# Strassen's algorithm for the states' first product, these tokens moved to the end, sums of w_in during batch 7

## Chip, cores, metric

The kernel runs on one core of one Trainium2 chip. The metric is the time on the device in microseconds. Most statements below need a second figure, the span that the profile gives from the core's first to last instruction; it lies 1.7 to 2.8 us under the time. All arithmetic here is float32 on TensorE.

## The reference

```python
# x: (8, 8, 512, 64), state: (8, 8, 32, 64), w_in: (512, 2048), w_out: (2048, 512)
a      = softmax(scale * x @ state.T)        # 512 tokens of a batch look at 32 states
xread  = a @ state
a2     = softmax(scale * state @ x.T)        # 32 states look at 512 tokens
sread  = a2 @ x
t      = concatenate([xread, sread])         # (8 batches * (512 + 32) tokens, 512)
h      = t @ w_in                            # the first product
out    = (h * sigmoid(1.702 * h)) @ w_out    # the second product
```

There are 8 x 512 "x tokens" and 8 x 32 = 256 "states' tokens". All 256 of these go through the two products together.

## The kernel before

The x tokens of batches 2 to 7 already use Strassen's algorithm (Winograd's form, 7 products and 15 sums) in both products; the states' tokens use it in the second product alone. Their first product is plain: 16 blocks of the hidden dimension, for each 4 matmul instructions over the 512 inputs, 256 columns wide.

```python
def up(key, f, ntok, lhs, rhs, spare=False):
    hps = ... psH.tile([P, ntok], FP32, tag="h", name=f"h_{key}_{f}")
    for i in range(n):                                   # n = 4 for the states
        nc.tensor.matmul(hps, lhs[i], rhs[i], start=(i == 0), stop=(i == n - 1))
    ...
    nc.scalar.activation(out=G[key, f // 2][:, f % 2, :ntok], in_=hps, func=AF.Gelu_apprx_sigmoid)

def up_s(f):
    up("sr", f, B * Ns, [w_in_of(k, f) for k in range(NPR)],
       [srT[:, k].rearrange("p b n -> p (b n)") for k in range(NPR)])
# ...
srT = konst.tile([P, NPR, B, Ns], FP32, name="srT")      # the states' tokens, batch by batch
# ... the end of the program:
for b in range(1, B):
    ahead = b + 1 < B
    if not ahead:                                        # the states ahead of batch 7
        for f in range(NF):
            up_s(f)
            ...                                          # sums for the second product
        strassen("sr", B * Ns, lambda r, n: out_s[nb * r.start : nb * r.stop, :, n])
    slots = att_slots(b + 1) if ahead else [[]]          # the next batch's attention, in 14 slots
    if b > 1:
        slots[0].insert(0, (up_strassen(b), ()))
    strassen(b, S, lambda r, n: out_x[b, r, :, n].rearrange("r q n -> q r n"), slots)
```

`strassen` is the second product: 7 products named by the PSUM bank in which they lie (x, y, x, y, z, y, z), a slot after every 8 instructions, and the sums of w_out made once. `up_strassen` is the first product of one batch; it leaves its last block of work to be done in slot 0, inside the second product.

Of the kernel before, what the change touches and what calls it, by code (L numbers as in the profile page):

```python
# [10 lines left out]
FP32 = mybir.dt.float32  # L11
# [3 lines left out]
ALU = mybir.AluOpType  # L15
# [5 lines left out]
def kernel(  # L21
# [30 lines left out]
    nc = tc.nc  # L52

    B, H, S, D = x.shape
# [179 lines left out]
        done["credit"] -= n  # L234
        round_to(done["b"] + n)

    def w_in_of(k, f):
        c, o = divmod(P * f, FC)
        return w_in[c][:, k, o : o + P]


    srT = konst.tile([P, NPR, B, Ns], FP32, name="srT")

# [174 lines left out]
    def up(key, f, ntok, lhs, rhs, spare=False):  # L418
        hps = att_ps([P, ntok], f"h_{key}_{f}") if spare else psH.tile([P, ntok], FP32, tag="h", name=f"h_{key}_{f}")
        n = len(lhs)  # L420
        for i in range(n):
            nc.tensor.matmul(hps, lhs[i], rhs[i], start=(i == 0), stop=(i == n - 1))  # L422
        if f % 2 == 0:
            G[key, f // 2] = free.pop(0)
        nc.scalar.activation(out=G[key, f // 2][:, f % 2, :ntok], in_=hps, func=AF.Gelu_apprx_sigmoid)  # L425
# [3 lines left out]
        m = A[b]["M", c]  # L429
        up(b, f, S, [m[:, g, o : o + P] for g in range(NG)], [A[b]["aT"][:, g] for g in range(NG)], spare)  # L430

    def up_s(f):
        up(
            "sr", f, B * Ns,
            [w_in_of(k, f) for k in range(NPR)],
            [srT[:, k].rearrange("p b n -> p (b n)") for k in range(NPR)],
        )

    O = {}

    def down(key, r, fs, dst, last):
# [19 lines left out]
    def quarters(key, u, ntok):  # L461

        g, half = G[key, u], ntok // 2
        return g[:, :, :half], g[:, :, half:ntok]

    def s12(key, u, ntok):

        half = ntok // 2
        (a11, a21), (_, a22) = quarters(key, u, ntok), quarters(key, HF // 2 + u, ntok)
        s1, s2 = S1[:, 2 * u : 2 * u + 2, :half], S2[:, 2 * u : 2 * u + 2, :half]  # L470
        nc.vector.tensor_tensor(out=s1, in0=a21, in1=a22, op=ALU.add)  # L471
        nc.vector.tensor_tensor(out=s2, in0=s1, in1=a11, op=ALU.subtract)

    def s3(key, u, ntok):

        a11, a21 = quarters(key, u, ntok)
        nc.vector.tensor_tensor(out=a21, in0=a11, in1=a21, op=ALU.subtract)

    def strassen(key, ntok, dst, slots=None):
        half = ntok // 2  # L480
        nb = half // P
        B11, B21, B22 = w_out[:, :HF, :HN], w_out[:, HF:, :HN], w_out[:, HF:, HN:]
        T3 = w_out[:, :HF, HN:]
        A = lambda i, k: [quarters(key, (HF * k + f) // 2, ntok)[i][:, f % 2] for f in range(HF)]
        S = lambda t: [t[:, f, :half] for f in range(HF)]
        todo = list(slots or [])

        def bank(name):
            return psO.tile([P, nb, HN], FP32, tag="o", name=f"{name}_{key}")

        def product(ps, lhs, rhs, first):
            for r in range(nb):
                for f in range(HF):
                    nc.tensor.matmul(  # L494
                        ps[:, r], lhs[f][:, P * r : P * (r + 1)], rhs[:, f],
                        start=(first and r == 0 and f == 0), stop=(f == HF - 1), skip_group_check=True,
                    )
                if todo:
                    for fn, args in todo.pop(0):
                        fn(*args)  # L500

        def kept(t):
            return t[:, : nb * HN].rearrange("p (r n) -> p r n", r=nb)

        def store(i, k, ps, with_):

            o = opool.tile([P, nb, HN], FP32, tag="osb", name=f"osb_{key}_{i}{k}")
            if with_ is None:
                nc.scalar.copy(o, ps)
            else:  # L510
                nc.vector.tensor_tensor(out=o, in0=ps, in1=with_, op=ALU.add)  # L511
            nc.sync.dma_start(dst(slice(nb * i, nb * (i + 1)), slice(HN * k, HN * (k + 1))), o)

        k1, k2, k3 = kept(p1), kept(u2), kept(u3)
        X = bank("x")
        product(X, A(0, 0), B11, True)
        nc.scalar.copy(k1, X)
        Y = bank("y")
        product(Y, S(S2), T2, True)
        nc.vector.tensor_tensor(out=k2, in0=Y, in1=k1, op=ALU.add)  # L520
        product(X, A(0, 1), B21, False)
        store(0, 0, X, None)
        for u in range(HF // 2):
            a12 = quarters(key, HF // 2 + u, ntok)[0]
            nc.vector.tensor_tensor(out=a12, in0=a12, in1=S2[:, 2 * u : 2 * u + 2, :half], op=ALU.subtract)
        product(Y, A(1, 0), T3, False)
        nc.vector.tensor_tensor(out=k3, in0=Y, in1=k1, op=ALU.add)
        free.extend(G[key, u] for u in range(HF // 2))
        Z = bank("z")
        product(Z, S(S1), T1, True)  # L530
        store(1, 1, Z, k3)
        product(Y, A(1, 1), T4, False)
        store(1, 0, Y, k1)
        product(Z, A(0, 1), B22, False)
        store(0, 1, Z, k2)
        free.extend(G[key, u] for u in range(HF // 2, HF))
# [23 lines left out]
            for c in range(2):  # L560
                nc.vector.tensor_tensor(out=t[:, c], in0=a["M", c][:, 1], in1=a["S2"][:, c], op=ALU.subtract)

    def up_strassen(b):

        a = A[b]
        b11, b22 = a["aT"][:, 0, :QT], a["aT"][:, 1, QT:]
        b21 = a["aT"][:, 1, :QT]
        t1, t2, t3, t4 = a["T"]
        banks = {}

        def product(u, bank, lhs, rhs, first):
            if first:
                pool, tag = (psH, "h") if bank == "x" else (psO, "o")
                banks[bank, u] = pool.tile([P, 2, QT], FP32, tag=tag, name=f"up{bank}_{b}_{u}")
            ps = banks[bank, u]
            for k in range(2):
                o = 2 * P * (u % 2) + P * k
                nc.tensor.matmul(  # L578
                    ps[:, k], lhs[:, o : o + P], rhs, start=(first and k == 0), stop=True, skip_group_check=True
                )  # L580
            return ps

        def gelu(dst, src):
            nc.scalar.activation(out=dst, in_=src, func=AF.Gelu_apprx_sigmoid)  # L584

        def add(ps, x, dst):
            nc.vector.tensor_tensor(out=dst, in0=ps, in1=x, op=ALU.add)  # L587

        def parts(u):
            c = u // 2  # L590
            return a["M", c], a["M", 2 + c], a["S1"][:, c], a["S2"][:, c], a["S4"][:, c]


        def begin(u):
            lo, hi, m1, m2, m4 = parts(u)
            G[b, u], G[b, NU + u] = free.pop(0), free.pop(0)
            _, c12 = quarters(b, u, S)
            c21, _ = quarters(b, NU + u, S)
            nc.scalar.copy(c21, product(u, "x", lo[:, 0], b11, True))
            add(product(u, "y", m2, t2, True), c21, c12)  # L600

        def middle(u):
            lo, hi, m1, m2, m4 = parts(u)
            c11, c12 = quarters(b, u, S)
            c21, c22 = quarters(b, NU + u, S)
            z = product(u, "z", m1, t1, True)
            gelu(c11, product(u, "x", lo[:, 1], b21, False))
            add(product(u, "y", hi[:, 0], t3, False), c21, c22)
            add(z, c22, c22)
            gelu(c22, c22)  # L610

        def end(u):
            lo, hi, m1, m2, m4 = parts(u)
            c11, c12 = quarters(b, u, S)
            c21, c22 = quarters(b, NU + u, S)
            add(product(u, "y", hi[:, 1], t4, False), c21, c21)
            gelu(c21, c21)
            add(product(u, "z", m4, b22, False), c12, c12)
            gelu(c12, c12)
            if u:  # L620
                s12(b, u - 1, S)

        for u in range(NU):
            begin(u)
            if u:
                end(u - 1)
            middle(u)

        def rest():
            end(NU - 1)  # L630
            s12(b, NU - 1, S)
            for u in range(NU):
                s3(b, u, S)

        return rest

# [112 lines left out]
    T_of(B12, B22, B12)  # L749
    T_of(T4, B21, T2)  # L750

    nb = P // Ns
    for b in range(1, B):
        ahead = b + 1 < B
        if not ahead:
            for f in range(NF):
                up_s(f)
                if f > HF and f % 2:
                    s12("sr", (f - HF) // 2, B * Ns)
                    s3("sr", (f - HF) // 2, B * Ns)  # L760
            strassen("sr", B * Ns, lambda r, n: out_s[nb * r.start : nb * r.stop, :, n])
        slots = att_slots(b + 1) if ahead else [[]]
        if b > 1:
            slots[0].insert(0, (up_strassen(b), ()))
        strassen(b, S, lambda r, n: out_x[b, r, :, n].rearrange("r q n -> q r n"), slots)
        if b + 2 < B:
            load_state(b + 2)
            load_x(b + 2)


# [28 lines left out]
```

## Time and profile before

| | before |
|---|---|
| time, three runs | 755.9, 756.31, 757.17 us |
| span of the profiled run | 755.7 us |
| TensorE / VectorE / ScalarE busy | 98% / 55% / 31% |
| states' first product | 128 records of 256 columns, 27.6 us |
| last store | 256 KB, 2.21 us from issue to last landing |

One thing is to be known about the times first: they are of two kinds. In some executions the trace has a stretch of 3413 ns at half clock some 41 to 43 us after the start, behind a pause of 2.1 us in which TensorE waits for ScalarE. The page of the profiled run before shows it only when asked for short stretches (columns: stretch, its length, busy time of PE, PEld, DVE, ACT and POOL with instructions, granted clock, share of the DMA engines, GB/s):

```profile
38.00:42.00 4.00, 1.98 (x17) 0.31 (x16) 3.93 (x7) 3.69 (x7) 0.00 (x0) 1.00 0.00 0
42.00:46.00 4.00, 3.90 (x6) 1.79 (x7) 3.90 (x9) 1.43 (x4) 0.00 (x0) 0.62 0.01 2
```

Executions with it have a mean clock of 0.996 to 0.998 and take about 1.7 us more; those without have 0.999 or 1.0. Both kinds are counted as fast. So I compare executions of the same kind, and call those without the stretch "clean".

### The profile page before, as it was taken

Reading aid. Unit: us, or ns where it says so; the run is one execution under the profiler, and the core shown is the slowest. Engines: PE = TensorE matmul, PEld = TensorE weight load, DVE = VectorE, ACT = ScalarE, POOL = GpSimd, SP = SyncE. Lnnn points to the kernel's source line nnn. Section 1 sums busy time; section 2 is a strip of 40 time slices with the busy share of each in tenths; the row PEclk is TensorE's granted clock in tenths of the full one; section 3 lists DMA queues with packets and bytes.
Section 4 is the critical chain, followed back from the end, with each engine's and each line's share of the span. In section 5 each row is a group of like instructions: output and inputs, shape, how many; then the busy total and the mean of one; then the engine's idle time right before and its main releaser. Section 6 shows DMA issues by size and latency. Waiting matters only on the chain.

```text
span 755.7 us, 9853 instructions
## 1 busy us (share of the span) xinstructions
PE 743.6 (98%) x4171; PEld 563.8 (75%) x4171; DVE 413.9 (55%) x712; ACT 231.7 (31%) x411; POOL 0.8 (0%) x8
## 2 busy tenths in 40 slices
PE   8989999999999999999999999999999999999997
PEld 3423454467888878887788788887888778888886
DVE  5999699632646373555637264638364550225511
ACT  4667611022324241433134232424142312104200
POOL 0000000000000000000000000000000000000000
PEclk9999999999999999999999999999999999999999
DMA  9811245010030000300030003000130000000001
GB/s 233 330 61 52 84 152 159 0 57 1 28 78 10 1 15 29 74 1 15 29 74 0 1 29 87 3 1 15 38 64 1 15 29 15 0 22 8 0 15 42
DMA packets 48763, 35.22 MB, mean 47 GB/s; under 512 B 36432, under 2 KB 44112, under 8 KB 48720
## 3 DMA queue, kind: packets, MB, share of 16 engines
q1 hardware_dynamic: 48720, 34.61, 15.9%
q8 instruction: 32, 0.52, 0.3%
q14 instruction: 11, 0.09, 0.0%
HBM read 25.69 MB, written 8.91 MB: 46 GB/s over the span
## 4 chain that ended last, share of the span: by engine, by line
PE 96%; SPq 2%; ACT 1%; DMA 1%; issue 0%; DVE 0%; ACTq 0%
PE y L494 19%; PE z L494 13%; PE x L494 13%; PE upy L578 8%; PE h L422 8%; PE o L447 7%; PE upx L578 5%; PE upz L578 5%; PE M L276 4%; PE h_sr L422 4%; PE xT L258 2%; PE y_sr L494 1%; SPq L131 1%; PE sr L371 1%; PE s L276 1%; PE z_sr L494 1%
## 5 line engine op out<-in xcount | busy, mean ns | idle before, releaser
L494 PE MATMUL x<-w_out,g 128*128 128x256 f32 x448 | 100.2, 379 | 0.0
L494 PEld LDWEIGHTS x<-w_out,g 128*128 128x128 f32 x448 | 84.2, 190 | 11.4 <-ACT osb L454 0.2
L587 DVE TENSOR_TENSOR g<-upy,g 128x512 f32<-128x512 f32 x72 | 48.1, 689 | 68.7 <-PE upy L578 68.7
L584 ACT ACTIVATE g<-g 128x512 f32<-128x512 f32 x72 | 44.8, 630 | 84.8 <-DVE g L587 84.8
L422 PE MATMUL h<-aT,M 128*128 128x512 f32 x128 | 59.9, 614 | 4.4 <-ACT M L351 4.4
L351 ACT COPY M<-M 128x512 f32<-128x512 f32 x64 | 33.2, 596 | 95.1 <-PE M L276 95.1
L422 PEld LDWEIGHTS h<-aT,M 128*128 128x128 f32 x128 | 24.2, 194 | 37.9 <-issue 25.5
L494 PE MATMUL z<-sums,later 128*128 128x256 f32 x224 | 51.1, 382 | 0.0
L494 PE MATMUL z<-w_out,g 128*128 128x256 f32 x224 | 50.8, 382 | 0.0
L494 PE MATMUL y<-sums,later 128*128 128x256 f32 x224 | 50.5, 379 | 0.0
L494 PE MATMUL y<-sums,g 128*128 128x256 f32 x224 | 50.5, 379 | 0.0
L494 PE MATMUL y<-w_out,g 128*128 128x256 f32 x224 | 50.1, 382 | 0.0
L494 PEld LDWEIGHTS y<-w_out,g 128*128 128x128 f32 x224 | 42.1, 190 | 10.5 <-issue 5.0
L494 PEld LDWEIGHTS z<-sums,later 128*128 128x128 f32 x224 | 42.1, 190 | 10.5 <-issue 5.0
L578 PE MATMUL upx<-aT,M 128*128 128x256 f32 x192 | 49.3, 379 | 0.0
L578 PE MATMUL upy<-ta,M 128*128 128x256 f32 x192 | 49.3, 379 | 0.0
L494 PEld LDWEIGHTS z<-w_out,g 128*128 128x128 f32 x224 | 41.6, 190 | 6.2
L494 PEld LDWEIGHTS y<-sums,g 128*128 128x128 f32 x224 | 41.6, 190 | 5.2
L494 PEld LDWEIGHTS y<-sums,later 128*128 128x128 f32 x224 | 41.6, 190 | 5.2
L471 DVE TENSOR_TENSOR later<-g,g 128x512 f32<-128x512 f32 (+1 forms) x32 | 20.8, 651 | 40.7 <-ACT g L425 40.7
L511 DVE TENSOR_TENSOR osb<-z,later 128x512 f32<-128x512 f32 x14 | 9.7, 692 | 60.2 <-PE z L494 60.2
L578 PEld LDWEIGHTS upx<-aT,M 128*128 128x128 f32 x192 | 36.5, 190 | 5.0
(130 smaller groups left out, 1023.0 us busy)
## 6 DMA issues: line engine op xcount, KB each, us to landing
later<-in_moe_w_out_dram SPq DMA_DIRECT2D x16, 512.0 KB
out_dram<-osb SPq DMA_DIRECT2D x32, 256.0 KB
xn<-in_x_dram SPq DMA_DIRECT2D x28, 256.0 KB
w_out<-in_moe_w_in_dram SPq DMA_DIRECT2D x12, 512.0 KB
later<-in_moe_w_in_dram SPq DMA_DIRECT2D x4, 512.0 KB
sums<-in_x_dram SPq DMA_DIRECT2D x4, 256.0 KB
stn<-in_state_dram SPq DMA_DIRECT2D x16, 32.0 KB
out_dram<-osb_sr SPq DMA_DIRECT2D x4, 128.0 KB
```

Of the source, the lines that this page charges most:

```text
L131: nc.sync.dma_start(xn[b][:, c], x_v[b, c])
L258: nc.tensor.transpose(ps[:, c], x_heads(b, c, j), ident)
L276: nc.tensor.matmul(ps[g][st], A[b]["stT"][rows, st], rhs(rows, j), start=True, stop=True)
L351: nc.scalar.copy(m[:, g], ps[g])
L422: nc.tensor.matmul(hps, lhs[i], rhs[i], start=(i == 0), stop=(i == n - 1))
L447: nc.tensor.matmul(ops, G[key, f // 2][:, f % 2, P * r : P * (r + 1)], w_out[:, f], start=(f == 0), stop=(f == NF - 1))
L471: nc.vector.tensor_tensor(out=s1, in0=a21, in1=a22, op=ALU.add)
L494: nc.tensor.matmul(ps[:, r], lhs[f][:, P * r : P * (r + 1)], rhs[:, f], start=(first and r == 0 and f == 0), stop=(f == HF - 1), skip_grou ...
L511: nc.vector.tensor_tensor(out=o, in0=ps, in1=with_, op=ALU.add)
L578: nc.tensor.matmul(ps[:, k], lhs[:, o : o + P], rhs, start=(first and k == 0), stop=True, skip_group_check=True)
L584: nc.scalar.activation(out=dst, in_=src, func=AF.Gelu_apprx_sigmoid)
L587: nc.vector.tensor_tensor(out=dst, in0=ps, in1=x, op=ALU.add)
```

## The change

The intent: 7 products in place of 8 for the states' first product as well. They need the four quarters of w_in added and subtracted; VectorE is to do that while TensorE works on batch 7. For this the states' tokens go behind batch 7, and `up_strassen` is made general (a list of pieces of the inner dimension, as the states have two where a batch has one). The diff, cut to its core:

```diff
+    def sr_sums():
+        mm = [mpool.tile([P, NG, FC], FP32, tag="M", name=f"ws_{i}") for i in range(4)]
+        s1, s2 = mm[:2], mm[2:]
+        ...                                             # s4 in xT, t1..t4 in e1, quarters of srT and w_in
+        for c in range(2):
+            steps.append((tt, (s1[c], hi[c][0], hi[c][1], ALU.add)))
+            steps.append((tt, (s2[c], s1[c], lo[c][0])))
+            steps.append((tt, (hi[c][0], lo[c][0], hi[c][0])))
+            steps.append((tt, (s4[c], lo[c][1], s2[c])))
+        steps += [(tt, v) for v in ((t1, r12, r11), (t2, r22, t1), (t3, r22, r12), (t4, r21, t2))]
@@ in product() of up_strassen
+            n = len(lhs)
             for k in range(2):
                 o = 2 * P * (u % 2) + P * k
-                nc.tensor.matmul(
-                    ps[:, k], lhs[:, o : o + P], rhs, start=(first and k == 0), stop=True, skip_group_check=True
-                )
+                for i in range(n):
+                    nc.tensor.matmul(
+                        ps[:, k], lhs[i][:, o : o + P], rhs[i],
+                        start=(first and k == 0 and i == 0), stop=(i == n - 1), skip_group_check=True,
+                    )
@@ the end of the program
         if not ahead:
-            for f in range(NF):
-                up_s(f)
-                ...
-            strassen("sr", B * Ns, lambda r, n: out_s[nb * r.start : nb * r.stop, :, n])
+            steps, left, right = sr_sums()
+            for i, step in enumerate(steps):
+                slots[1 + i].append(step)
         strassen(b, S, lambda r, n: out_x[b, r, :, n].rearrange("r q n -> q r n"), slots)
...
+    strassen(
+        "sr", B * Ns, lambda r, n: out_s[nb * r.start : nb * r.stop, :, n],
+        [[(up_strassen("sr", B * Ns, left, right), ())]],
+    )
```

More of the change, by code (lines that the diff above doesn't have):

```diff
@@ L235, in pace @@
         round_to(done["b"] + n)
-    def w_in_of(k, f):
-        c, o = divmod(P * f, FC)
-        return w_in[c][:, k, o : o + P]
     srT = konst.tile([P, NPR, B, Ns], FP32, name="srT")
@@ L430, in up_x @@
         up(b, f, S, [m[:, g, o : o + P] for g in range(NG)], [A[b]["aT"][:, g] for g in range(NG)], spare)
-    def up_s(f):
-        up(
-            "sr", f, B * Ns,
-            [w_in_of(k, f) for k in range(NPR)],
-            [srT[:, k].rearrange("p b n -> p (b n)") for k in range(NPR)],
-        )
     O = {}
@@ L561, in up_sums, with parts_x, left @@
                 nc.vector.tensor_tensor(out=t[:, c], in0=a["M", c][:, 1], in1=a["S2"][:, c], op=ALU.subtract)
-    def up_strassen(b):
+    def parts_x(b):
         a = A[b]
-        b11, b22 = a["aT"][:, 0, :QT], a["aT"][:, 1, QT:]
-        b21 = a["aT"][:, 1, :QT]
-        t1, t2, t3, t4 = a["T"]
+        t1, t2, t3, t4 = ([t] for t in a["T"])
+        r11, r21, r22 = [a["aT"][:, 0, :QT]], [a["aT"][:, 1, :QT]], [a["aT"][:, 1, QT:]]
+        def left(u):
+            c = u // 2
+            lo, hi = a["M", c], a["M", 2 + c]
+            return [lo[:, 0]], [lo[:, 1]], [hi[:, 0]], [hi[:, 1]], [a["S1"][:, c]], [a["S2"][:, c]], [a["S4"][:, c]]
+        return left, (r11, r21, r22, t1, t2, t3, t4)
@@ new lines, in sr_sums, with tt, each, left @@
+    def sr_sums():
+        HT, HK = B * Ns // 2, NPR // 2
+        mm = [mpool.tile([P, NG, FC], FP32, tag="M", name=f"ws_{i}") for i in range(4)]
+        s1, s2 = mm[:2], mm[2:]
+        t = apool.tile([P, NPR, S], FP32, tag="xT", name="ws4")
+        s4 = [t[:, HK * c : HK * (c + 1)] for c in range(2)]
+        t = apool.tile([P, NG, NB, Ns], FP32, tag="e1", name="ta_sr").rearrange("p g i n -> p (g i n)")
+        t1, t2, t3, t4 = ts = [t[:, HK * HT * i : HK * HT * (i + 1)].rearrange("p (k t) -> p k t", k=HK) for i in range(4)]
+        sT = srT.rearrange("p k b n -> p k (b n)")
+        r11, r12, r21, r22 = (sT[:, HK * i : HK * (i + 1), HT * k : HT * (k + 1)] for i in range(2) for k in range(2))
+        lo = [[w_in[c][:, HK * i : HK * (i + 1)] for i in range(2)] for c in range(2)]
+        hi = [[w_in[2 + c][:, HK * i : HK * (i + 1)] for i in range(2)] for c in range(2)]
+        def tt(out, x0, x1, op=ALU.subtract):
+            nc.vector.tensor_tensor(out=out, in0=x0, in1=x1, op=op)
+        steps = []
+        for c in range(2):
[4 more added lines that the diff above has]
+        steps += [(tt, v) for v in ((t1, r12, r11), (t2, r22, t1), (t3, r22, r12), (t4, r21, t2))]
+        def each(v):
+            return [v[:, k] for k in range(HK)]
+        def left(u):
+            c = u // 2
+            return [each(v) for v in (lo[c][0], lo[c][1], hi[c][0], hi[c][1], s1[c], s2[c], s4[c])]
+        return steps, left, [each(v) for v in (r11, r21, r22, *ts)]
@@ L569, in up_strassen @@
+    def up_strassen(b, ntok, left, right):
+        QT = ntok // 2
+        b11, b21, b22, t1, t2, t3, t4 = right
         banks = {}
@@ L575, in product @@
             ps = banks[bank, u]
+            n = len(lhs)
             for k in range(2):
                 o = 2 * P * (u % 2) + P * k
-                nc.tensor.matmul(
-                    ps[:, k], lhs[:, o : o + P], rhs, start=(first and k == 0), stop=True, skip_group_check=True
-                )
+                for i in range(n):
[3 more added lines that the diff above has]
+                    )
             return ps
@@ L587, in add @@
             nc.vector.tensor_tensor(out=dst, in0=ps, in1=x, op=ALU.add)
-        def parts(u):
-            c = u // 2
-            return a["M", c], a["M", 2 + c], a["S1"][:, c], a["S2"][:, c], a["S4"][:, c]
         def begin(u):
-            lo, hi, m1, m2, m4 = parts(u)
+            l11, l12, l21, l22, m1, m2, m4 = left(u)
             G[b, u], G[b, NU + u] = free.pop(0), free.pop(0)
-            _, c12 = quarters(b, u, S)
-            c21, _ = quarters(b, NU + u, S)
-            nc.scalar.copy(c21, product(u, "x", lo[:, 0], b11, True))
+            _, c12 = quarters(b, u, ntok)
+            c21, _ = quarters(b, NU + u, ntok)
+            nc.scalar.copy(c21, product(u, "x", l11, b11, True))
             add(product(u, "y", m2, t2, True), c21, c12)
         def middle(u):
-            lo, hi, m1, m2, m4 = parts(u)
-            c11, c12 = quarters(b, u, S)
-            c21, c22 = quarters(b, NU + u, S)
+            l11, l12, l21, l22, m1, m2, m4 = left(u)
+            c11, c12 = quarters(b, u, ntok)
+            c21, c22 = quarters(b, NU + u, ntok)
             z = product(u, "z", m1, t1, True)
-            gelu(c11, product(u, "x", lo[:, 1], b21, False))
-            add(product(u, "y", hi[:, 0], t3, False), c21, c22)
+            gelu(c11, product(u, "x", l12, b21, False))
+            add(product(u, "y", l21, t3, False), c21, c22)
             add(z, c22, c22)
@@ L612, in end @@
         def end(u):
-            lo, hi, m1, m2, m4 = parts(u)
-            c11, c12 = quarters(b, u, S)
-            c21, c22 = quarters(b, NU + u, S)
-            add(product(u, "y", hi[:, 1], t4, False), c21, c21)
+            l11, l12, l21, l22, m1, m2, m4 = left(u)
+            c11, c12 = quarters(b, u, ntok)
+            c21, c22 = quarters(b, NU + u, ntok)
+            add(product(u, "y", l22, t4, False), c21, c21)
             gelu(c21, c21)
@@ L620, in end @@
             if u:
-                s12(b, u - 1, S)
+                s12(b, u - 1, ntok)
         for u in range(NU):
@@ L630, in rest @@
             end(NU - 1)
-            s12(b, NU - 1, S)
+            s12(b, NU - 1, ntok)
             for u in range(NU):
-                s3(b, u, S)
+                s3(b, u, ntok)
         return rest
@@ L750 @@
     T_of(T4, B21, T2)
-    nb = P // Ns
     for b in range(1, B):
         ahead = b + 1 < B
+        slots = att_slots(b + 1) if ahead else [[] for _ in range(14)]
+        if b > 1:
+            slots[0].insert(0, (up_strassen(b, S, *parts_x(b)), ()))
         if not ahead:
-            for f in range(NF):
-                up_s(f)
-                if f > HF and f % 2:
-                    s12("sr", (f - HF) // 2, B * Ns)
-                    s3("sr", (f - HF) // 2, B * Ns)
-            strassen("sr", B * Ns, lambda r, n: out_s[nb * r.start : nb * r.stop, :, n])
-        slots = att_slots(b + 1) if ahead else [[]]
-        if b > 1:
-            slots[0].insert(0, (up_strassen(b), ()))
+            steps, left, right = sr_sums()
+            for i, step in enumerate(steps):
+                slots[1 + i].append(step)
         strassen(b, S, lambda r, n: out_x[b, r, :, n].rearrange("r q n -> q r n"), slots)
@@ L768 @@
             load_x(b + 2)
+    nb = P // Ns
+    strassen(
+        "sr", B * Ns, lambda r, n: out_s[nb * r.start : nb * r.stop, :, n],
+        [[(up_strassen("sr", B * Ns, left, right), ())]],
+    )
 _INS = ['x', 'state', 'moe_w_in', 'moe_w_out']
```

## The prediction

> **What bounds the kernel now.** I read the page's busy table first, then the chain of work that ended last over the final 127 us, then the groups kept apart by shape, then the timeline of single transitions, and last the DMA view of the final store.
>
> ```profile
> PE 743.6 (98%) x4171; PEld 563.8 (75%) x4171; DVE 413.9 (55%) x712; ACT 231.7 (31%) x411; POOL 0.8 (0%) x8
> ...
> PEclk9999999999999999999999999999999999999999
> ```
>
> TensorE is busy 98% of 755.7 us at full clock; no other engine comes near. Busy alone proves little, because matmul records overlap, so the chain has to confirm it:
>
> ```profile
> 629.88 25.04 PE h_sr L422 x116
> 654.91 3.45 PE x_sr L494 x16
> ...
> 675.63 3.45 PE z_sr L494 x16
> 679.09 0.86 PE upx L578 x4
> ...
> 744.70 6.92 PE z L494 x32
> 751.62 0.02 issue
> 751.64 0.69 DVE osb L511
> ```
>
> Columns: start, length, engine, product, records. From the first record of the states' first product (h_sr) to the last addition there is only TensorE, without a gap. So a record removed from this stretch is time removed from the kernel, and a record added is time added. The pitch of a 256-column float32 record is 3.45/16 = 0.2157 us (the 379 ns in the groups is latency, not pitch). One matmul instruction leaves two records: 64 instructions in the source, 128 records here:
>
> ```profile
> L422 PE MATMUL h_sr<-srT,w_in 128*128 128x256 f32 x128 | 27.8, 379 | 0.0
> ...
> L422 PEld LDWEIGHTS h_sr<-srT,w_in 128*128 128x128 f32 x128 | 24.3, 190 | 3.3
> ```
>
> Each record has its own weight load, recorded with 190 ns.
>
> **What the Trainium skill says, and whether the trace agrees.** (1) "TensorE: Matmul & The Clock Gate", section "Back-to-back issue gap", gives N/2.4 + 2.5 ns between warm matmuls, so 109 ns for 256 columns; the trace has 216 ns, twice that, and float32 is not treated there. I read a float32 record as two cycles a column: 512/2.4 + 2.5 = 216 (estimate from that formula). For 128 columns that makes 109 ns. (2) The same page, section "LDWEIGHTS (loading the stationary operand)", gives P/1.2, 107 ns for 128 columns. So at 128 columns matmul and load would tie, and this tie is the heart of the prediction. (3) "VectorE: DVE Perf Modes", section "The TRN2 errata", gives (N+151)/0.96 ns for a float32 addition of two tensors: 1224 ns at N = 1024; the trace's 128x1024 subtraction takes 1225 ns, and 425 ns at N = 256 fits too. (4) "DMA: Bandwidth & Descriptors", section "Why a DMA increments its semaphore by 16 and not by 1", says a transfer uses the largest number of engines up to 16 that divides its slowest dimension. The states' stores have 4 batches there, so 4 engines; the trace agrees below.
>
> **The pitch of 128-column records.** The old kernel has none in a plain float32 product, but it has the pieces:
>
> ```profile
> 165.08 0.47 PEld L258 LDWEIGHTS xT<-ident,xn 128*128 128x128 f32 x4
> 165.19 0.60 PE L258 MATMUL xT<-ident,xn 128*128 128x128 f32 x4
> ...
> 620.00 0.30 PEld L494 LDWEIGHTS z<-w_out,g 128*128 128x128 f32 x2
> ```
>
> Four 128-column transposes cover 0.60 us, one lasts 0.273, so three pitches are 0.327: 109 ns each, with a weight load each. Transposes load faster (141 ns recorded), so they do not settle it. The last line is two ordinary float32 loads after a pause: together 0.30, one is 0.19, so they start 108 ns apart although each is recorded as 190. Loads thus follow each other at 108 ns, the matmul at 109. I choose 109 ns.
>
> **The change part by part.**
> Removed: 64 instructions x 2 records x 0.2157 = 27.6 us.
> Added: 7 products x 4 blocks x 2 halves of rows x 2 parts of K = 112 instructions, 224 records of 128 columns: 224 x 0.109 = 24.4 us. Seven products instead of eight at half the width each: 7/8 of 27.6 is 24.2, the rest is the fixed 2.5 ns per record. **On the path: -3.2 us.**
> Additions in the new product: per block 5 additions of 256 elements on VectorE (0.42), one copy and four gelus on ScalarE (0.37 to 0.39); with the sums for the second product about 32 x 0.42 = 13.5 us of VectorE and 20 x 0.38 = 7.6 us of ScalarE in 24 us. The x tokens' version runs the same order with operations of 0.69 and 0.63 us at the same 0.86 us per product and TensorE never waits there; here a product takes 8 x 0.109 = 0.87. Beside other work: 0.
> Sums of w_in: 8 additions of 1024 elements, 8 x 1.225 = 9.8 us, and 4 of the tokens, 4 x 0.42 = 1.7: 11.5 us on VectorE during batch 7's second product (about 50 us, VectorE 2 to 5 tenths busy early and 1 later). No product needs an answer from VectorE there sooner than one 6.9 us product later, and a slot puts at most one or two sums ahead of it. Beside: 0.
> Moved: batch 7 now follows batch 6 as batches 2 to 6 follow theirs; those crossings show no TensorE wait. 0.
> The new handover from first to second product: the x tokens cover the last block's additions with the second half of product X; the states' X has only 8 instructions, so Y follows at once. Y needs the last block's sums only at its seventh instruction, 6 x 0.43 = 2.6 us in. The chain is addition, gelu, four more additions in order: 0.25 + 0.43 + 4 x 0.4 = about 2.3 us, and the weights are fetched one record early. About even; I add 0.1 us.
> The end: the last addition falls from 0.69 to 0.42, -0.27. The last store changes from 256 KB of x tokens to 128 KB of states, but on fewer engines:
>
> ```profile
> GB/s 0 0 0 0 0 0 0 0 0 0 0 0 11 42 53 32 11 21 74 105 84 95 95 95 105 95 95 95 105 95 42 0 0 0 0 0 0 0 0 0
> ...
> GB/s 0 0 0 0 0 0 0 0 0 0 0 87 298 335 372 335 348 335 372 348 261 87 0 0 0 0 0 0 0 0 0 0 0 0 0 0 0 0 0 0
> ```
>
> First the last states' store (window 679.5 to 683.4 us), then the last x store (752.3 to 755.6). The half-sized store runs at some 95 GB/s and not 340; from issue to the last landing it takes 3.29 us, against 2.21. In the old kernel that was hidden behind batch 7, in the new one it is the end. **+1.08, with the addition +0.8 us.**
> Sum: -3.2 + 0.8 + 0.1 = -2.3 us; 756.3 - 2.3 = **754.0 us**, 0.3% faster.
>
> **The rivals.**
> A. Weight loads become the bound. For it: 190 ns recorded per load, and the tie leaves no slack; that page's section "Back-to-back issue gap" also reports 81 ns in a stream of load and matmul where the isolated gap is 56. Against it: loads seen 108 ns apart. At 141 ns per record the product would take 31.6 us and the kernel 761; at 190 ns, 42.6 us and 772, the only way to a 2% loss.
> B. The short states' products expose VectorE and ScalarE: at the handover, or in the new first product. For it: TensorE's order has no other work to fill with, and the handover is even. Against it: operations shrink by 40% at equal product length. At 0.5 us in each place, 755.
> C. The sums of w_in delay an addition that TensorE waits for in batch 7. Against it: 11.5 us of work in 50 us with slack of 6.9. At worst 1 us, 755.
> D. The store costs no more than the x store after all: 753.
>
> **Range and chances.** C, B and D move the time by about 1 us each around 754.0, the runs before differ by 1.3 us, and a pitch of 115 ns instead of 109 would cost 1.3 us more. Range 752.8 to 756.8, open upward because of A. No way leads to 741, so faster by over 2% gets 0.01; slower by over 2% needs the worst of A, 0.03; within 2%, 0.96.
>
> **What would show it.** Right: 224 records of the states' up products at 0.109 us pitch, about 24.4 us from first to last; no TensorE wait for VectorE or ScalarE over 0.2 us in the last 50 us; VectorE some 11 us busier in batch 7 with TensorE unbroken; the last landing about 3.7 us after the last addition begins, against 2.9 before. Wrong: a pitch of 120 ns or more for 128-column records (A); waits of product Y's loads at the handover (B); an idle TensorE during batch 7's second product (C). If the span falls by 3 us or more, the last store was mis-sized.

## The result

The changed kernel took 754.28 us in the median of all four runs (754.23 in that of the three fast ones), where the kernel before took 756.2. The ratio is 0.9972 with an interval of 0.9953 to 0.9992. (Ratios here are the mean time of one kernel's fast runs over that of the other's in the same rounds, so not quite the ratio of the medians.) One of the four runs took 1308.46 us at a mean clock of 0.557; it is left out of everything that follows. The time lies inside the predicted range.

The three fast runs after were all clean, those before were mixed, which flatters the change. Over all runs, clean ones alone, the mean span of the kernel before is 753.99 us (12 runs) and of the changed kernel 752.44 us (5 runs): **1.55 us less, not 2.3.** That is the number to be explained. It is good to a few tenths: in times, the clean runs differ by 1.70 us (755.93 and 754.23), and in the one later job that ran both kernels on one chip the spans differ by 1.7 in clean runs and by 1.2 in the others.

The profile after, first the busy table:

```profile
PE 738.5 (98%) x4265; PEld 564.6 (75%) x4267; DVE 432.5 (57%) x744; ACT 233.1 (31%) x415; POOL 0.8 (0%) x8
```

VectorE has 18.6 us more to do, TensorE is as full as it was. The chain of work that ended last, from the crossing into the states' tokens on (start, length, engine, product, records):

```profile
691.28 6.91 PE z L483 x32
698.19 0.89 PE upx_sr L614 x8
699.08 0.89 PE upy_sr L614 x8
...
720.52 0.89 PE upy_sr L614 x8
721.41 3.46 PE x_sr L483 x16
724.87 0.89 PE upy_sr L614 x8
725.76 0.89 PE upz_sr L614 x8
726.65 3.46 PE y_sr L483 x16
...
743.92 3.47 PE z_sr L483 x16
747.39 0.02 issue
747.41 0.42 DVE osb_sr L500
```

Again only TensorE, no gap at the crossing, none at the handover to product Y at 726.65, and the wait table of TensorE from 640 us on is empty. But a product of 8 records takes 0.89 us, not 0.87: from 698.19 to 726.65 less the 3.46 of x_sr there are 25.0 us for 224 records, so their pitch, the time from one record's start to the next one's, is 111.7 ns.

The groups by shape show the new product's matmuls (latency 275 ns) and their loads:

```profile
L614 PE MATMUL upx_sr<-srT,w_in 128*128 128x128 f32 x64 | 8.5, 275 | 0.0
...
L614 PEld LDWEIGHTS upx_sr<-srT,w_in 128*128 128x128 f32 x64 | 7.9, 192 | 0.1
```

From the first record of batch 2's first product to the last matmul of the program the profiled run before has 532.17 us (its half-clock stretch lies ahead of batch 2) and the clean run after 529.55: 2.61 less, as the two products differ (27.63 and 25.01). So TensorE's part is accounted for in full, and the rest is behind it. From the start of the last matmul to the end of the span there were 4.44 us, now 5.55. The parts, from the traces:

| | before | after |
|---|---|---|
| start of the last matmul to start of the last addition | 0.42 | 0.41 |
| start of the last addition to issue of the store | 0.72 | 0.45 |
| issue to last landing | 2.21 | 3.30 |
| last landing to end | 1.10 | 1.39 |

-2.61 + 1.11 = -1.50, against -1.55 between the means of clean runs. The third row is the store on few engines, seen in the DMA view of the last 4.3 us (GB/s in 40 slices):

```profile
GB/s 0 0 0 0 0 0 0 0 0 0 0 0 38 48 19 29 19 86 86 95 86 86 95 105 86 114 76 114 38 0 0 0 0 0 0 0 0 0 0 0
```

The fourth row was foreseen by nobody.

### The profile page after: what moved, and what is told of

It is laid out like the page before. It is cut to its first block, busy times and chain, and to the rows that moved or that the text cites. A ratio compares the mean times of both kernels' runs of the same rounds, so it can differ in the third digit from the quotient of the medians.

```text
span 752.6 us, 10076 instructions
## 1 busy us (share of the span) xinstructions
PE 738.5 (98%) x4265; PEld 564.6 (75%) x4267; DVE 432.5 (57%) x744; ACT 233.1 (31%) x415; POOL 0.8 (0%) x8
## 4 chain that ended last, share of the span: by engine, by line
PE 96%; SPq 2%; ACT 1%; DMA 1%; issue 0%; DVE 0%; ACTq 0%
PE y L483 19%; PE z L483 13%; PE x L483 13%; PE upy L614 8%; PE h L418 8%; PE o L436 7%; PE upz L614 6%; PE upx L614 6%; PE M L272 4%; PE xT L254 2%; PE upy_sr L614 1%; PE y_sr L483 1%; SPq L131 1%; PE sr L367 1%; PE s L272 1%; PE upz_sr L614 1%
## 5 line engine op out<-in xcount | busy, mean ns | idle before, releaser
L621 ACT ACTIVATE g<-g 128x512 f32<-128x512 f32 (+1 forms) x84 | 49.8, 600 | 100.5 <-DVE g L624 100.5
L418 PE MATMUL h<-aT,M 128*128 128x512 f32 x128 | 58.2, 600 | 4.4 <-ACT M L347 4.4
L418 PEld LDWEIGHTS h<-aT,M 128*128 128x128 f32 x128 | 23.6, 190 | 36.7 <-issue 24.4
L614 PEld LDWEIGHTS upy<-ta,M 128*128 128x128 f32 x192 | 36.5, 190 | 4.9
```

The costliest lines, as they stand in the source:

```text
L614: nc.tensor.matmul(ps[:, k], lhs[i][:, o : o + P], rhs[i], start=(first and k == 0 and i == 0), stop=(i == n - 1), skip_group_check=True,)
L621: nc.scalar.activation(out=dst, in_=src, func=AF.Gelu_apprx_sigmoid)
```

## The experiments

Theory: the change saves 2.6 us of TensorE, which are 3.2 less a loss because the weight loads set the pitch; the sums are free where they are; the end gives 0.8 back by its store and 0.3 by something else. Rivals: the order and not the algorithm brings the gain; the pitch is a matmul's own; sums or handover cost something that the trace hides. The expectations speak of times; where the kinds of run are mixed I give clean spans as well.

### The changed kernel again, on another chip

No edit.

> The changed kernel once more, so that the other runs of this chip can be set against it. Theory (first product 2.6 us shorter at the measured pitch of 111.7 ns, end 0.8 us longer): 1.8 us below the kernel before, ratio 0.9976. Rival (the 2 us are mostly luck of the start): ratio 0.999 or more.

Ratio 0.9981 (0.9966 to 0.9995). Clean runs 754.17 and 754.21 us; the four others, with the half-clock stretch, 755.97 to 757.02. The medians of this job, 757.35 before and 756.01 after, differ from the first job's mainly by the mixture: the clean runs after agree within 0.2 us. The difference holds up on another chip. The ratio makes it 1.4 us (0.4 to 2.6), the clean spans alone 1.7; the expected 1.8 lies inside the noise, although the fourth row of the table above was not yet in its sum.

### The order alone

```diff
     for b in range(1, B):
         ahead = b + 1 < B
-        if not ahead:
-            for f in range(NF):
-                up_s(f)
-                ...
-            strassen("sr", ...)
         ...
+    for f in range(NF):
+        up_s(f)
+        ...
+    strassen("sr", ...)
```

> The states' tokens last of all, but with the old plain product of 64 instructions, no sums. Theory: only the end changes, last addition 0.27 us shorter and last store 1.08 us longer, so 0.8 us above the kernel before, about 757.0, ratio 1.001. Rival D of the prediction (the short store costs no more at the end): 0.3 us below before, ratio 0.9996. Rival (the new order alone brings the gain, by sparing a crossing): 754 to 755.

Ratio 1.0007 (0.9993 to 1.0021). Clean span 754.90 us (3 runs), 0.91 above the clean span before, 0.78 above that of the same chip. The end of the chain, with the plain product of 27.63 us now behind batch 7:

```profile
699.40 27.63 PE h_sr L422 x128
...
747.75 3.47 PE z_sr L494 x16
751.21 0.02 issue
751.24 0.42 DVE osb_sr L511
```

The trace has 0.45 us from last addition to issue and 3.29 from issue to landing, as in the changed kernel, and 1.10 us after it. So the order alone costs 0.8 to 0.9 us, and the algorithm alone brings 754.90 - 752.44 = 2.46 us. The rivals (order brings the gain; short store is cheap at the end) fall.

### The last store on 16 engines

```diff
-    srT = konst.tile([P, NPR, B, Ns], FP32, name="srT")
+    srT = konst.tile([P, NPR, Ns, B], FP32, name="srT")
-        nc.scalar.copy(srT[:, :, b, :], ps.rearrange("p (j n) -> p j n", j=NPR))
+        nc.scalar.copy(srT[:, :, :, b], ps.rearrange("p (j n) -> p j n", j=NPR))
-        "sr", B * Ns, lambda r, n: out_s[nb * r.start : nb * r.stop, :, n],
+        "sr", B * Ns, lambda r, n: out_s.rearrange("b t d -> t b d")[P // B * r.start : P // B * r.stop, :, n],
```

(and the flattening of srT in `sr_sums` to match). A store now has 16 states outside and 8 batches inside, where it had 4 batches outside and 32 states inside.

> The changed kernel with the states' tokens laid out state by state and batch inside, so that a store's slowest dimension is 16 and not 4. Theory: the last store runs on 16 engines, from issue to last landing about 1.8 to 2.2 us where it was 3.30, so 1.1 to 1.5 us below the changed kernel: about 753.0, ratio to before 0.996. Rival (the store's length is set by its 1 KB rows or its latency, not by the number of engines): no change, ratio 0.9975.

Ratio 0.9967 (0.9953 to 0.9981), one clean run of 751.4 us. The last store, in the DMA view of the last 3.7 us:

```profile
GB/s 0 0 0 0 0 0 0 0 0 0 0 0 0 111 177 177 210 277 299 133 33 0 0 0 0 0 0 0 0 0 0 0 0 0 0 0 0 0 0 0
```

It reaches 300 GB/s where it had about 100, and 16 landings are counted where there were 5, the first of these ahead of any data. From issue to last landing it takes 2.28 us, not 3.30: 1.02 less, just short of what I expected (1.1 to 1.5). Between these two sizes the bytes hardly count: on 16 engines half the bytes of the x tokens' store take 2.28 us, the whole 2.21.

### The same layout in the kernel before

The same edit in the kernel before (its own flattening of srT in `up_s`).

> The kernel before with the same layout of the states' tokens: its stores get faster too, but they end some 70 us ahead of the end. Theory (hidden): no change, ratio 1.000 within 0.0005. Rival (the layout itself gains or costs, by the copy with stride 8 or by the matmuls' reading): a shift of 0.5 us or more.

Ratio 0.9998 (0.9982 to 1.0013), clean span 753.7 us (one run). In its trace the last of these stores lands 2.28 us after its issue, where it took 3.29 before. The faster stores lie beside batch 7 and are worth nothing there; the layout itself costs nothing. The same stores matter only where they are last.

### 96 columns in every second instruction

```diff
+                    w = 96 if b == "sr" and i else QT
                     nc.tensor.matmul(
-                        ps[:, k], lhs[i][:, o : o + P], rhs[i],
+                        ps[:, k, :w], lhs[i][:, o : o + P], rhs[i][:, :w],
```

Its output is wrong, which doesn't matter for the time.

> The changed kernel with only 96 of 128 columns streamed in every second instruction of the states' first product (wrong results on purpose). Theory (the weight load sets the pitch): the 112 short records stay at about 111.7 ns, the time does not change. Rival (the matmul's columns set it, with a few ns more per record): 96 columns take 2 x 96/2.4 + 2.5 = 82.5 ns (estimate from the 215.8 ns of 256 columns), so 27 to 29 ns less on 112 records, 3.1 us off the time.

Ratio 0.9969 (0.9951 to 0.9988); clean runs 754.14 and 754.25 us, as the changed kernel's. The timeline of TensorE in this run:

```profile
701.29 1.06 PE L615 MATMUL upz_sr<-ta_sr,ws 128*128 128x128 f32 x8
702.19 1.06 PE L615 MATMUL upx_sr<-srT,w_in 128*128 128x128 f32 x8
703.08 1.06 PE L615 MATMUL upy_sr<-ta_sr,w_in 128*128 128x128 f32 x8
703.98 1.06 PE L615 MATMUL upx_sr<-srT,w_in 128*128 128x128 f32 x8
```

Products still start 0.89 us apart although half of their records stream a quarter less. So the matmuls' columns don't set the pitch. Single records show what does. In this run matmuls start at 702.327, .439, .524, .635 and .774, that is 112, 85, 111 and 139 ns apart, in a pattern that repeats; the weight loads start at 702.329, .441, .553, .664 and .776, every 111 to 112 ns all the same. The loads keep the pace and the matmuls follow them.

The first trace after shows the same pace: a load starts at 701.600, the next at 701.713, the next at 701.824, and a matmul 109 to 110 ns behind its load. My two numbers, 108 ns for loads and 109 for matmuls, came from a pair of loads after a pause and from transposes; neither was a stream of ordinary float32 loads, and in such a stream the loads come every 111.7 ns. What is not shown: no run shortens the loads themselves, so that it is a load's length, and not another fixed cost of each record with its load, is argued.

### The sums of w_in twice

```diff
-            for i, step in enumerate(steps):
-                slots[1 + i].append(step)
+            for i, (fn, v) in enumerate(steps):
+                slots[1 + i].append((fn, v))
+                if i < 8:
+                    slots[1 + i].append(steps[i - 1 if i % 4 == 2 else i])
```

(The third sum of each four overwrites its own input, so that its predecessor is repeated instead.)

> The changed kernel with each of the eight sums of w_in computed twice in its slot (same results). Theory (they lie beside the second product of batch 7): 9.8 us more of VectorE, the time as the changed kernel's within 0.3 us, 754.3. Rival C (sums delay additions that TensorE waits for): waits of TensorE for VectorE in batch 7, 1 us or more.

Ratio 0.9968 (0.9949 to 0.9988); clean runs 753.96 and 754.15 us. In equally placed stretches of 58 us, first the changed kernel, then this one:

```profile
643.50:701.50 58.00, 58.00 (x286) 51.56 (x285) 28.12 (x40) 6.37 (x11) 0.00 (x0) 1.00 0.06 19
```

```profile
645.00:703.00 58.00, 58.00 (x284) 51.44 (x283) 37.42 (x48) 6.37 (x11) 0.00 (x0) 1.00 0.06 19
```

VectorE has 9.3 us more to do, TensorE is busy for all 58.00 us in both. Batch 7 has room for twice the sums. The 0.1 to 0.2 us by which this kernel is even faster fit the end of its trace: 1.10 us from last landing to end instead of 1.39.

### The sums behind batch 7's last matmul

```diff
-                slots[1 + i].append(step)
+                slots[13].append(step)
```

> The changed kernel with all twelve sums put behind the last matmul of batch 7, ahead of its last addition. Theory (their place is what hides them): the last addition of batch 7 and the states' second product wait for 9.8 + 1.7 us of VectorE less what the first blocks do without them; TensorE idles, mostly ahead of the first products with sums, 8 to 12 us, so about 764. Rival (VectorE has room there too, because the last products of batch 7 leave it idle and the program runs ahead): less than 2 us.

Ratio 1.0031 (1.0012 to 1.0049); the four spans are 757.7 to 758.1 us, 5.3 and more above the clean changed kernel. The profiled run, of 757.7, has no half-clock stretch near its start, so it may be set against clean runs; of the other three the start is not kept. I had said 8 to 12. The timeline shows why it is less: VectorE starts the sums as soon as its own queue allows, at 691.70, during the last product of batch 7 and 6 us ahead of the states' first record. The wait for them, and what came after it:

```profile
PE upy_sr L614 <- DVE ta_sr L580: 3.3, 1, 3.3
```

```profile
697.70:702.05 4.35, 1.10 (x9) 0.91 (x9) 4.32 (x6) 0.37 (x1) 0.00 (x0) 1.00 0.00 0
702.05:703.50 1.45, 1.45 (x13) 1.45 (x13) 1.34 (x4) 0.00 (x0) 0.00 (x0) 0.97 0.00 0
703.50:707.00 3.50, 3.50 (x20) 3.50 (x19) 0.21 (x1) 0.38 (x1) 0.00 (x0) 0.52 0.22 75
707.00:710.00 3.00, 3.00 (x29) 3.00 (x28) 1.27 (x3) 0.68 (x2) 0.00 (x0) 1.00 0.01 3
```

TensorE idles 3.25 us, and then has half its clock (0.52 in the third stretch) for 3413 ns. From batch 2's first record to the last matmul there are 534.67 us and not 529.55, 5.12 more: the first record that needs a sum starts 3.4 us late, and the half clock costs 1.7. The Trainium skill's page "TensorE: Matmul & The Clock Gate", Part 1, describes a halved clock after an idle window of 3413 ns; the length agrees to the nanosecond, but only 2.04 us of this pause fall into the 3413 ns before the clock drops (see the closing list). So in the profiled run the place of the sums is worth 5 us, more than the whole algorithm brings; going by the closing list, 1.7 of it depend on how the pause lies to those windows.

### The 16-engine store again, with and without eight tiny instructions

```diff
                 slots[1 + i].append(step)
+                if i < 8:
+                    slots[1 + i].append((nc.vector.memset, (one, 1.0)))
```

> The version with the states' stores on 16 engines once more, beside its variant with eight tiny instructions. Theory: 1.0 us below the changed kernel like for like, last landing 2.28 us after issue, and 1.39 us from there to the end, as in its first run. Ratio to before 0.9965.

> The same with eight one-element memsets on VectorE in the slots of the sums in batch 7. The traces show a fetch of 8192 bytes of instructions within the last microsecond of the runs in which 1.39 us lie between the last landing and the end, and none there where it is 1.10 us (one of these has eight VectorE instructions more). Theory (an instruction fetch at the very end costs 0.29 us, and eight more instructions move it away): 1.10 us from last landing to end, 0.3 us faster than without. Rival (the 0.29 us come from something else): 1.39 us again, same time.

Without: ratio 0.9964 (0.995 to 0.9978), clean span 751.52 us (4 runs), in the trace 2.28 us to the landing and 1.39 from there. With: ratio 0.9974 (0.996 to 0.9987), but four of its five runs had the half-clock stretch; the clean one has 751.3 us. In the trace the end behaves as the theory says: 1.10 us from last landing to end, and a fetch of 8192 bytes of instructions (a packet on the instruction queue, not a data queue) that stood at the very end now stands at 740.0 us. Two cautions. My expectation put this fetch "within the last microsecond"; looked at closely, its packet starts 0.3 to 0.6 us after the last instruction's end, in all five traces that have the 1.39 us. What lies inside the span is a closing instruction of VectorE that starts 0.35 us late. That asking for the fetch holds VectorE up is thus a guess; shown is that eight instructions more move both away together. And in the times: the runs with the half-clock stretch have a mean span of 752.92 us, against 753.12 in the five such runs of the version without (both jobs), 0.2 less, but the single clean run of 751.3 us is no faster than the clean ones without. The times alone don't show it.

### One link more at the handover

```diff
             if u:
                 s12(b, u - 1, ntok)
+                if b == "sr" and u == NU - 1:
+                    s12(b, u - 1, ntok)
```

> The changed kernel with the two additions of the third block's sums done twice at the handover to the states' second product (same results). In the changed kernel the last sum ends 0.17 us ahead of the weight load that needs it. Theory (the handover has next to no slack): TensorE waits 0.6 to 0.8 us in product Y of the states, the time rises by as much. Rival (the weight loads or the queue have more room than the trace shows): no wait.

Ratio 0.9994 (0.9977 to 1.0011). In the changed kernel, the timeline at the handover reads:

```profile
726.49 2.97 PE L483 MATMUL y_sr<-sums,later 128*128 128x256 f32 x13
...
727.48 0.42 DVE L461 TENSOR_TENSOR later<-later,g 128x256 f32<-128x256 f32 x1
...
728.28 0.42 DVE L461 TENSOR_TENSOR later<-later,g 128x256 f32<-128x256 f32 x1
```

The last sum ends at 728.70, and the load of the seventh instruction, which reads it, starts at 728.87. There is a second such pair, and I had overlooked it: the third block's sum ends at 727.91, and the load of the fifth instruction, which reads that one, starts at 728.01, only 0.10 us later. It is this sum that the experiment makes twice:

```profile
729.91 0.43 DVE L461 TENSOR_TENSOR later<-later,g 128x256 f32<-128x256 f32 x1
...
730.39 0.98 PEld L483 LDWEIGHTS y_sr<-sums,later 128*128 128x128 f32 x5 [0.90 <-DVE later L461]
```

With these two additions more, 0.80 us of VectorE, the fifth instruction's load waits, the matmuls come 0.77 us late, and from batch 2's first record to the last matmul there are 530.32 us and not 529.55. The end of this trace gives 0.29 back (1.10 us after the landing, not 1.39). The times don't settle how much of it is left: the one clean run has 753.2 us, 0.8 above the changed kernel, the other three 754.5 to 754.6, where the changed kernel has 754.2 to 755.2. The handover has 0.10 us to spare at the fifth instruction and 0.17 at the seventh, and no more; the chain's theory holds.

## Why the prediction was right

The range held, and every place where TensorE was said not to wait was found without a wait. The size was off by a third like for like, -1.5 against -2.3, by terms that partly cancel. By the prediction's steps:

- **Bound by TensorE: right.** The 2.61 us that the records got shorter are the 2.61 us that the whole stretch got shorter.
- **The pitch, "I choose 109 ns": mis-sized.** It is 111.7, and the new product takes 25.0 us, not 24.4: the saving is 2.6, not 3.2. The tie was seen, and the larger of the two was rightly taken; but the 108 ns for loads was read from two loads after a pause, and in a stream they come every 111.7 ns, longer than the matmul's 109. Rival A is thus true in kind (the matmuls' columns don't set the pitch, the loads keep it, as the run with 96 columns shows) and small in size.
- **Additions and gelus beside the new product: right**, no wait; halving their size kept them ahead of products equally long.
- **The sums of w_in beside batch 7: right**; doubled, they still cost nothing. Rival C falls. Put later they cost 5 us.
- **The handover, +0.1: a hair too much.** There is no wait, with 0.17 us to spare at the seventh instruction; "about even" was right, as the lengthened chain shows. What the prediction didn't see is the fifth instruction, with 0.10 us the nearer one.
- **The end, +0.8: right** (0.72 to 0.45 and 2.21 to 3.30 makes +0.82). Rival D falls with the order alone. What was missing was the 0.29 us after the landing, of which the profile before gives no sign.
- **The reference, 756.3: a mixture** of runs with and without the half-clock stretch. That 754.0 came so near to 754.28 is in part luck: the three fast runs after were clean, and their gain was counted from a level about 0.4 us above the clean one (755.93). Errors of +0.6 (pitch), +0.3 (after the landing), -0.1 (handover) and -0.4 (reference) partly cancelled.

The best version that ran is the changed kernel with the states' tokens laid out for 16 engines: 0.9964 of the time before, 751.5 us of clean span.

## What to carry to other kernels

Before moving work to the end of a program, look at the landing of its last store, not at its size: 128 KB on few engines took 1.1 us longer than 256 KB on 16, and that was hidden until the store became the last. When matmuls get narrower, compare their time with the pitch of weight loads, measured in a stream of loads of the same type and not on a pair after a pause; a fifth of Strassen's 3.2 us went there. And sums that are free in a slack stretch cost, when they are put where TensorE waits, what nothing covers of their length (3.4 of some 11.5 us here) and, on top, the clock that TensorE loses in the pause (1.7 us).

## What the Trainium skill lacked or had wrong

- "TensorE: Matmul & The Clock Gate", "Back-to-back issue gap": the section has no figures for float32. A float32 instruction leaves two records, each with a load; 256 columns run at 215.8 ns a record, and 128 columns at 111.7 ns with 96 columns no faster.
- The same page, "LDWEIGHTS (loading the stationary operand)": its 107 ns for 128 columns comes close (109 to 110 ns from a load's start to its matmul's), but it does not say that float32 loads in a stream follow each other at 111.7 ns, nor that a load is recorded with 190.
- The same page, Part 1: the halved clock of 3413 ns agrees, but the window before it need not be idle throughout. In the twelve kept traces all stretches of full and half clock before the last half-clock one are whole multiples of 3413.3 ns (37547 is 11 of them, 706559 is 207, 747519 is 219). Cut into such windows, each window in which TensorE idled 1.67 us or more was followed by half clock, and none in which it idled 1.58 us or less. This separates the two kinds of run: in the seven traces with the stretch, 1.67 to 2.12 us of idle time near the start lie in one window, in the five clean ones a border cuts the pause of 2.1 us, and no window there has over 1.58. The pause of 3.25 us in the run with late sums lay in two windows, with 1.21 and 2.04 us.
- "DMA: Bandwidth & Descriptors", "Anatomy of one DMA": 2.0 us plus bytes over 436 GB/s gives 2.3 us for 128 KB, as on 16 engines (2.28). But the section gives that fit for DMAs that GpSimd issues, and these stores come from SyncE, for which the page has no such fit; nor does the fit go with the number of engines (3.30 us on 4).
- No page has this: in the traces with a fetch of 8192 bytes of instructions right after the end, 1.39 us lay between the last landing and the end, in those with it elsewhere or without it 1.10.
